# Tile 1's comparisons moved ahead of tile 0's sums, another place for half of a weight, and a changed order of subtractions

## The chip, the cores and the metric

The kernel runs on one core of one Trainium2 chip. The metric is the device time of one execution in microseconds. The core has five engines, each with a queue of its own that it works through in order: TensorE (PE, matrix multiplications), VectorE (DVE), ScalarE (ACT), GpSimd (POOL) and SyncE (SP, which here only issues transfers). An instruction may wait for other engines' work by semaphores, and what stands behind it on its engine then waits too.

## The reference, cut to what matters

An input x of 2048 rows by 512 goes through two branches, mixed by a gate g = sigmoid(x · gate_w):

```python
# branch A: linear attention, 32 heads of 16 features
q, k, v = split(x @ wqkv)
phi_q = concat(softmax(q @ w_phi), softmax(-(q @ w_phi)))     # 32 features a head; phi_k alike
kv, z = phi_k^T @ v, sum(phi_k over rows)
a = ((phi_q @ kv) / (phi_q @ z + 1e-6)) @ wo
# branch B: 32 heads, each picks one of 16 x 16 experts
s1, s2 = (x @ w_q) @ k1, (x @ w_q) @ k2                       # 16 scores each
expert = (argmax(s1), argmax(s2))                             # softmax over one choice is 1
b = sum over heads of gelu(x · u[expert]) * v[expert]
out = g * a + (1 - g) * b
```

What is computed must be seen in one respect: branch B is done by counting. For each row and expert the number of heads that chose it is counted (from the comparisons "score equals the row's largest"), and the counts, multiplied by gelu(x @ u^T), go into one matrix product with v.

## The kernel before, in words

The 2048 rows are 16 tiles of 128. Every float32 product is three products of parts: a number is split into a high part, which a copy rounds, and a low part, the difference (xh and xl for x, wbh and wbl for a weight, and so on).

**First stage** (lines 324 to 579): for each tile the key features, their softmax, the values, and the accumulation of kv (`kvacc`), beside the loading and turning of w_q. From tile 5 on the loop at line 463 takes tiles in pairs t and t+1 and saves products by adding and subtracting parts of x. The rows that matter here, for the pair (t, t+1):
- `x_high` (ScalarE, from tile 3 on) and `x_low` (VectorE, L156) split the tiles t+2 and t+3 before they are needed.
- `k_diffs` (VectorE, four operations L115 to L121) forms a tile's differences to the row's largest and least key feature, reading the product from PSUM; `behind` is the second tile of the pair before, whose differences are made here. `k_exp` (ScalarE L267), `k_sum` (VectorE L271, L272) and `k_mult` (GpSimd L276) finish the softmax.
- `Sums.add(t + 2)` (GpSimd, L175 to L178) adds and subtracts the raw tiles t+2 and t+3 in place, so it must wait until both have been split; `Sums.high` and `Sums.low` (L183, L189) split the results into gh, gl and the places of x15, which TensorE uses in the next pair (`pe`, `pu`).
- Copies of PSUM by ScalarE (L481, L505, L530) start new accumulations from old ones; TensorE waits for them.

**Second stage** (loop at line 944). Pass a does, for tile a, the query features and their softmax (`soft_in`, `soft_exp`, `soft_w`, `soft_sum`, `soft_y`, `soft_p`, `soft_b`); for tile n = a+1, the expert scores (`front_s`, in two halves), the comparisons of each half (`best`: L706 finds each head's largest score, L707 compares) and the transpose of their result by a transfer (`turn_eq`, L713, to `et`); for tile b = a-1, the planes of the softmax that are turned by transfers (`planes`, `join` to `pt`) and the end of the counting; for tile z = a-2 the last products (`back`). `mid_mask(a)` multiplies et with a small matrix (`mk`), from which VectorE counts.

The counting chain (`count`, lines 772 to 808) is a row of some seventeen small VectorE operations on tiles A, B, m, X and T, each of which needs the one before. `step(t, n)` issues n of its links, and so deals them in between other VectorE work; `soft_b` takes a link between each two of its operations, and `dealt` gives five, five and two places between the four operations of the next tile's `soft_in`.

The output weight wo is loaded and split in this stage: two quarters before the loop (`wo_load((0, 1))`), two in pass 0. The high parts are copied by ScalarE (L980), the low parts subtracted by GpSimd (L1006); quarters 0 and 1 go to t1h and t1l, 2 and 3 to the places of the value weights wbh and wbl (quarters 2 and 3 of them), which are free once `vproj(NT - 1)`, the values of the last tile, has been computed in pass 1. The copy of these values (`v15`, L255) releases `kvacc(NT - 1)`.

The order on each engine is the order of the calls in the source, written out by hand. Tiles in pools bring waits: a new tile on an old place waits for that place's last users. The pool `late` holds the key features of every other pair (tag "d", two places) and is closed in pass 1; `w4`, with `pt`, then takes its room.

Of the kernel before, what the change touches and what calls it, by code (L numbers as in the profile page):

```python
# [20 lines left out]
P = 128  # L21
S = 2048
D = 512
# [12 lines left out]
def mix_kernel(ctx, tc, xT, wqT, wkT, wv, wphi, wo, wq, kk, ug, ev, cst, out):  # L36
# [229 lines left out]
    def k_exp(t):  # L266
        act.activation(phis[t], phis[t], AF.Exp)  # L267
# [195 lines left out]
    for t in range(5, NT - 1, 2):  # L463
        n = t + 1
        more = [u for u in (t + 4, t + 5) if u < NT]
        for u in more:
            x_load(u)
        if t == NT - 5:
            rawu = [spare(ug[:, 0:2], "rawu0", [P, 2, NU])]
        elif t == NT - 3:  # L470
            rawu.append(spare(ug[:, 2:4], "rawu1", [P, 2, NU]))
            rawe = [spare(ev[:, 0], "rawe0", [P, D])]
        for u in (t + 2, t + 3):
            if u < NT - 1:
                x_low(u)
        if behind:
            k_diffs(behind)
        a = pks[t] = mm_bank(f"pk{t}")
        prod(a, tile_of(t, 0), b11, True)
        b = mm_bank(f"pu{t}")  # L480
        act.copy(b, a)  # L481
        if 5 < t < NT - 3:
            Sums.add(t + 2)
        if t == 5:
            (j1, tp), = joins
            joins.clear()
            tj1 = wa_.tile([P, D], F32, tag="wtj", bufs=1, name="wtj1")
            join_tp(j1, tp, tj1)
            score_planes(2)
            load_wq()  # L490
            load_wq()
            join_end(j1, tj1)
            Sums.add(t + 2)
        elif t < NT - 3:
            join_all()
        else:
            (j6, tp), = joins
            joins.clear()
            tj6 = wa_.tile([P, D], F32, tag="wtj", bufs=1, name="wtj6")
            join_tp(j6, tp, tj6)  # L500
        e = tr_bank(f"pe{t}")
        prod(e, sums(0, 2), b1, True)
        prod(b, sums(1, 0), b2, False)
        c = mm_bank(f"pv{t}")
        act.copy(c, b)  # L505
        if t == 5:
            k_exp(4)
            k_sum(4)
            k_mult(4)
            join_all()  # L510
        prod(a, tile_of(t, 2), b21, False)
        k_diffs(t)
        if behind:
            k_exp(behind)
            k_sum(behind)
            k_mult(behind)
        score(1)
        if t == NT - 3:
            rawq = stage(wqT, "rawq")
        score(1)  # L520
        for u in (t - 3, t - 2):
            kvacc(u)
        vn, vt = v_tile(n), v_tile(t)
        if t > 5:
            act.copy(vn, by16(e))
            k_exp(t)
            k_sum(t)
        prod(b, sums(0, 0), b3, False)
        d = pks[n] = mm_bank(f"pk{n}")
        act.copy(d, b)  # L530
        if t == 5:
            k_exp(t)
            k_sum(t)
            act.copy(vn, by16(e))
        prod(c, sums(1, 2), b22, False)
        if t == NT - 3:
            x_split(NT - 1)
        dve.tensor_tensor(vt, by16(c), vn, op=ALU.add)
        dve.tensor_tensor(vn, by16(b), vn, op=ALU.add)
        o2 = d.rearrange("p (c n) -> p c n", c=2)  # L540
        prod(o2, tile_of(n, 2), b4, False)
        if t + 3 < NT:
            Sums.high(t + 2)
            Sums.low(t + 2)
        if t == 7:
            for i in range(2):
                x_parts(i, 11)
        for u in more if n < NT - 4 else ():
            x_high(u)
        k_mult(t)  # L550
        behind = n
    t = NT - 1
# [295 lines left out]
        ch, cl, o = st8[t]["c"]  # L848
        eng.tensor_tensor(cl, o[:, :2 * P], ch, op=ALU.subtract)

    woh = [(t1h if k < 2 else wbh)[:, k] for k in range(NK)]
    wol = [(t1l if k < 2 else wbl)[:, k] for k in range(NK)]

    def back_mm(t, cols=slice(0, D), bank=None):
        e = st8[t]
# [43 lines left out]
            pe.matmul(o, neg, zl[:, s_], start=False, stop=True)  # L899
            act.copy(zb[:, s_], o)  # L900

    def wo_load(ks):
        for k in ks:
            rawo[k] = w3.tile([P, D], F32, tag="ot", name=f"rawo{k}")
            sp.dma_start(rawo[k], wo[:, k, :])

    rawo = {}
    kvacc(NT - 2)
# [20 lines left out]
    mid_mask(0)  # L929
    z_final()  # L930
    gelu_rest(0)
    wo_load((0, 1))
    def dealt(a, b, z):
        def first():
            for _ in gate(a):
# [8 lines left out]
    for a in range(NT - 1):  # L944
# [5 lines left out]
            mid_num(z)  # L950
        if a == 2:
            gelu_pre(a)
        if B:
            planes(b, 0)
            if Z:
                c_join(z)
            planes(b, 1)
            front_q(a)
        if owed:
            back(z - 1, owed)  # L960
            store(z - 1)
        if a == 1:
            v15 = vproj(NT - 1)
        gelu_in(a)
        if Z:
            num_lo(z)
        if B:
# [7 lines left out]
        gelu_act(a)  # L975
        if a > 0:
            soft_exp(a)
        if a < 2:
            for k in (2 * a, 2 * a + 1):
                act.copy(woh[k], rawo[k])  # L980
        if Z and not left:
            back(z)
# [17 lines left out]
        soft_sum(a, 0)  # L1000
        soft_sum(a, 1)
        if a == 0:
            step(a, 8)
        if a < 2:
            for k in (2 * a, 2 * a + 1):
                pool.tensor_tensor(wol[k], rawo[k], woh[k], op=ALU.subtract)  # L1006
        if a == 0:
            wo_load((2, 3))
        best(n, 0)
        soft_y(a, 0)  # L1010
        soft_y(a, 1)
        soft_p(a)
        if B:
# [1 line left out]
            gelu_out(b)  # L1015
            coef(b)
            c_planes(b)
        soft_b(a)
        best(n, 1)
        turn_eq(n)  # L1020
        if a != 1:
            gelu_pre(n)
    a, b, z = NT - 1, NT - 2, NT - 3
# [122 lines left out]
```

## Time and profile before

| | |
|---|---|
| median of 3 runs | 376.59 us (376.45 to 376.63) |
| the profiled execution | 376.26 us |
| its span, first to last instruction | 374.5 us |
| TensorE busy | 365.2 us |
| VectorE busy | 334.1 us |
| ScalarE busy | 256.7 us |
| GpSimd busy | 206.3 us |
| bytes read from and written to memory | 26.43 MB, 4.19 MB |

The profile is of one execution. Times are microseconds from its first instruction. A row of the timeline gives the start, the duration, the engine, the line (L56 is line 56), the operation, output and inputs by name, sizes, and how many such operations the row holds; in brackets stands the idle time of the engine ahead of it and what ended it. Durations overlap: a matmul is recorded with 0.39 us, but the next starts 0.23 us after it. A row of the waits gives who waited for what: microseconds in all, times, the longest.

### The profile page before, as it was taken

Reading aid. Unit: us, or ns where it says so; the run is one execution under the profiler, and the core shown is the slowest. Engines: PE = TensorE matmul, PEld = TensorE weight load, DVE = VectorE, ACT = ScalarE, POOL = GpSimd, SP = SyncE. Lnnn points to the kernel's source line nnn. Section 1 sums busy time; section 2 is a strip of 40 time slices with the busy share of each in tenths; the row PEclk is TensorE's granted clock in tenths of the full one; section 3 lists DMA queues with packets and bytes.
Section 4 is the critical chain, followed back from the end, with each engine's and each line's share of the span. In section 5 each row is a group of like instructions: output and inputs, shape, how many; then the busy total and the mean of one; then the engine's idle time right before and its main releaser. Section 6 shows DMA issues by size and latency. Waiting matters only on the chain.

```text
span 374.5 us, 8838 instructions
## 1 busy us (share of the span) xinstructions
PE 365.2 (98%) x3443; PEld 285.7 (76%) x3443; DVE 334.1 (89%) x784; ACT 256.7 (69%) x458; POOL 206.3 (55%) x206
## 2 busy tenths in 40 slices
PE   8999999999999998999999999999999999999995
PEld 4766776667878886778888878888778888888875
DVE  4679898999877989999999999999999999999993
ACT  5576678776576674878759568677786787687741
POOL 1089989799838745844535427335445454454700
PEclk9999999999999999999999999999999999999999
DMA  7967887757981124244253242453553532532201
GB/s 273 330 243 244 302 273 188 255 170 196 265 184 35 21 68 112 45 87 97 71 86 87 70 98 60 98 80 35 113 60 82 114 70 72 115 63 65 72 31 56
DMA packets 72218, 46.67 MB, mean 125 GB/s; under 512 B 63600, under 2 KB 64496, under 8 KB 69872
## 3 DMA queue, kind: packets, MB, share of 16 engines
q1 hardware_dynamic: 71312, 45.24, 47.0%
q10 hardware_dynamic: 864, 0.87, 0.8%
q8 instruction: 27, 0.44, 0.5%
q14 instruction: 15, 0.12, 0.1%
HBM read 26.43 MB, written 4.19 MB: 82 GB/s over the span
## 4 chain that ended last, share of the span: by engine, by line
PE 76%; DVE 7%; ACT 5%; issue 4%; DMA 3%; POOL 3%; POOLq 0%; ACTq 0%; DVEq 0%
PE po L861 10%; PE s L56 6%; PE s L57 6%; PE s L58 6%; PE po L868 5%; PE pq L56 4%; PE pk L453 3%; PE pq L58 3%; PE pq L57 3%; PE ws L292 3%; PE oT L749 2%; PE pu L453 2%; PE kvacc L283 2%; PE pp L57 2%; PE pp L58 2%
## 5 line engine op out<-in xcount | busy, mean ns | idle before, releaser
L663 POOL TENSOR_TENSOR w<-d,zb 128x512 f32<-128x512 f32 x32 | 41.0, 1297 | 78.3 <-ACT d L657 78.3
L56 PE MATMUL s<-sh,xh 128*128 128x512 f32 x128 | 50.8, 397 | 0.0
L57 PE MATMUL s<-sl,xh 128*128 128x512 f32 x128 | 49.9, 390 | 0.0
L58 PE MATMUL s<-sh,xl 128*128 128x512 f32 x128 | 49.8, 389 | 0.0
L698 POOL TENSOR_TENSOR d<-d,st 128x512 f32<-128x512 f32 x30 | 31.2, 1063 | 27.6 <-DVE st L692 25.6
L657 ACT ACTIVATE d<-d 128x512 f32<-128x512 f32 x32 | 20.1, 634 | 32.9 <-DVE d L119 24.8
L276 POOL TENSOR_TENSOR d<-d,st 128x1024 f32<-128x1024 f32 x16 | 33.6, 2101 | 13.3 <-DVE st L272 9.3
L740 ACT COPY pt<-tp 128x1024 uint16<-128x1024 uint16 x28 | 36.3, 1366 | 0.0
L730 ACT COPY pl<-d 128x1024 uint16<-128x1024 uint16 x28 | 29.2, 1045 | 9.1 <-POOL d L698 9.1
L58 PEld LDWEIGHTS s<-sh,xl 128*128 128x128 f32 x128 | 24.0, 188 | 5.0
L56 PEld LDWEIGHTS s<-sh,xh 128*128 128x128 f32 x128 | 24.0, 188 | 4.7
L57 PEld LDWEIGHTS s<-sl,xh 128*128 128x128 f32 x128 | 24.1, 188 | 4.6
L56 PE MATMUL pq<-wah,xh 128*128 128x512 f32 x64 | 26.8, 418 | 0.0
L58 PE MATMUL pq<-wah,xl 128*128 128x512 f32 x64 | 25.1, 392 | 0.0
L57 PE MATMUL pq<-wal,xh 128*128 128x512 f32 x64 | 25.0, 390 | 0.0
L271 DVE TENSOR_REDUCE st<-d 128x64 f32<-128x1024 f32 x16 | 19.4, 1212 | 5.1 <-ACT d L267 4.9
L707 DVE TENSOR_TENSOR eq<-s,mx 128x512 bf16<-128x512 f32 x32 | 22.1, 692 | 1.1
L667 DVE TENSOR_REDUCE st<-d 128x32 f32<-128x512 f32 x32 | 21.6, 683 | 1.6
L267 ACT ACTIVATE d<-d 128x1024 f32<-128x1024 f32 x16 | 17.0, 1065 | 7.6 <-DVE d L121 7.6
L156 DVE TENSOR_TENSOR xl<-xr,xh 128x512 fp32r<-128x512 f32 (+2 forms) x17 | 20.7, 1239 | 1.5 <-ACT xh L152 1.4
L706 DVE TENSOR_REDUCE mx<-s 128x32 f32<-128x512 f32 x32 | 21.8, 682 | 0.0
L677 DVE TENSOR_REDUCE st<-w 128x32 f32<-128x512 f32 x32 | 20.5, 677 | 0.6 <-POOL w L663 0.5
(258 smaller groups left out, 1119.9 us busy)
## 6 DMA issues: line engine op xcount, KB each, us to landing
wq<-wq SPq DMA_DIRECT2D x16, 1024.0 KB, 5.6
xr<-xT SPq DMA_DIRECT2D x15, 256.0 KB, 3.9
y<-ot SPq DMA_DIRECT2D x15, 256.0 KB, 2.3
rawk<-wkT SPq DMA_DIRECT2D x1, 1024.0 KB, 6.0
rawq<-wqT SPq DMA_DIRECT2D x1, 1024.0 KB, 6.7
rawo<-wo SPq DMA_DIRECT2D x4, 256.0 KB, 3.7
rawu<-ug SPq DMA_DIRECT2D x2, 258.0 KB, 4.2
rawv<-wv ACTq DMA_DIRECT2D x2, 256.0 KB, 4.5
```

What stands on the lines that cost most here:

```text
L56: pe.matmul(o, ah, bh, start=(first and i == 0), stop=False)
L57: pe.matmul(o, ah, bl, start=False, stop=False)
L58: pe.matmul(o, al, bh, start=False, stop=(last and i == n - 1))
L276: pool.tensor_tensor(g64(d), g64(d), b64(st[:, 128:192]), op=ALU.mult)
L663: pool.tensor_tensor(hs(e["w"], i), hs(e["ph"], i), hs(zb, i), op=ALU.mult)
L667: dve.tensor_reduce(pair(e["st"][:, 64:128])[:, :, i], hs(e["ph"], i), axis=AX.X, op=ALU.add)
L698: eng.tensor_tensor(g64(d)[:, gs_], g64(d)[:, gs_], r[:, gs_].unsqueeze(2).to_broadcast([P, 32, F]), op=ALU.mult)
L706: dve.tensor_reduce(mx, p3, axis=AX.X, op=ALU.max)
L707: dve.tensor_tensor(e["eq"][:, 512 * half:512 * half + 512].rearrange("p (h f) -> p h f", f=F), p3, mx.unsqueeze(2).to_broadcast([P, H, F] ...
L730: act.copy(pl, e["ph"][:, halves[i]].bitcast(U16).rearrange("p (c j) -> p j c", j=2))
L740: act.copy(p16[:, :, 4 * i:4 * i + 4, :], e["tp"][i].rearrange("p (j g) n -> p j g n", j=2))
L861: pe.matmul(po, a, b, start=(i == 0), stop=False)
```

## The change

Three things change, all of them the order or the place of work; what is computed stays the same.

1. In the pair loop, `k_diffs(behind)` stands ahead of the two `x_low`. For tile 9 alone both splits are taken out of this and moved into the pair (5, 6): the high behind the multiplication of tile 4, the low between the exponential and the sum of tile 5.
2. wo's second half is loaded as one transfer of 512 KB right after the first two quarters, onto a place of the pool `late` that held key features; it is split in pass 1, right after the last tile's values, ahead of `planes` on ScalarE and ahead of `soft_w` on GpSimd, and goes to the first two quarters of wbh and wbl.
3. In pass 0, `best(1, 0)`, `best(1, 1)` and `turn_eq(1)` come earlier, ahead of the sums `soft_y`. Seven links of tile 0's counting chain are dealt around them (3, 2, 2) instead of eight ahead, and `soft_b(0)` takes none, so ten are left for pass 1 where four were.

```diff
-        for u in (t + 2, t + 3):
-            if u < NT - 1:
-                x_low(u)
         if behind:
             k_diffs(behind)
+        for u in (t + 2, t + 3):
+            if u < NT - 1 and u != 9:
+                x_low(u)
...
             k_mult(4)
+            x_high(9)
             join_all()
...
             k_exp(t)
+            x_low(9)
             k_sum(t)
...
         for u in more if n < NT - 4 else ():
-            x_high(u)
+            if u != 9:
+                x_high(u)
...
-    woh = [(t1h if k < 2 else wbh)[:, k] for k in range(NK)]
-    wol = [(t1l if k < 2 else wbl)[:, k] for k in range(NK)]
+    woh = [(t1h if k < 2 else wbh)[:, k % 2] for k in range(NK)]
+    wol = [(t1l if k < 2 else wbl)[:, k % 2] for k in range(NK)]
...
-    def wo_load(ks):
-        for k in ks:
+    def wo_load():
+        for k in range(2):
             rawo[k] = w3.tile([P, D], F32, tag="ot", name=f"rawo{k}")
             sp.dma_start(rawo[k], wo[:, k, :])
+        both = late.tile([P, 2, D], F32, tag="d", name="rawo2")
+        sp.dma_start(both, wo[:, 2:4, :])
+        rawo.update({2: both[:, 0], 3: both[:, 1]})
...
+        if a == 1:
+            front_q(a)
+            v15 = vproj(NT - 1)
+            for k in (2, 3):
+                act.copy(woh[k], rawo[k])
         if B:
             planes(b, 0)
             if Z:
                 c_join(z)
             planes(b, 1)
+        if a > 1:
             front_q(a)
...
+        gelu_in(a)
         if a == 1:
-            v15 = vproj(NT - 1)
-        gelu_in(a)
+            for k in (2, 3):
+                pool.tensor_tensor(wol[k], rawo[k], woh[k], op=ALU.subtract)
...
-        if a < 2:
-            for k in (2 * a, 2 * a + 1):
+        if a == 0:
+            for k in range(2):
                 act.copy(woh[k], rawo[k])
...
         soft_sum(a, 0)
         soft_sum(a, 1)
         if a == 0:
-            step(a, 8)
-        if a < 2:
-            for k in (2 * a, 2 * a + 1):
+            for k in range(2):
                 pool.tensor_tensor(wol[k], rawo[k], woh[k], op=ALU.subtract)
+            step(a, 3)
+        best(n, 0)
         if a == 0:
-            wo_load((2, 3))
-        best(n, 0)
+            step(a, 2)
+            best(n, 1)
+            turn_eq(n)
         soft_y(a, 0)
+        if a == 0:
+            step(a, 2)
         soft_y(a, 1)
         soft_p(a)
...
-        soft_b(a)
-        best(n, 1)
-        turn_eq(n)
+        if a == 0:
+            soft_b(a, lambda t: None)
+        else:
+            soft_b(a)
+            best(n, 1)
+            turn_eq(n)
```

Where the rows come to stand, on the engines concerned. Line numbers of the changed kernel are 3 higher from line 511 on, and up to 19 higher at the end.

VectorE in the first stage, at the end of the pair (5, 6) and the start of (7, 8), before (d_762 and d_806 are the differences of tiles 6 and 7, xr_576 and xr_578 the raw tiles 9 and 10):

```order
L271 TENSOR_REDUCE st_637<-d_636 128x64
L272 RECIPROCAL st_637<-st_637 128x64
L538 TENSOR_TENSOR v_721<-pv_620,v_719 128x32x16
L539 TENSOR_TENSOR v_719<-pu_589,v_719 128x32x16
L156 TENSOR_TENSOR xl_68<-xr_576,xh_65 128x512
L156 TENSOR_TENSOR xl_68<-xr_578,xh_65 128x512
L115 TENSOR_REDUCE st_763<-pk_729 128x32
L117 TENSOR_REDUCE st_763<-pk_729 128x32
L119 TENSOR_TENSOR d_762<-pk_729,st_763 128x32x16
L121 TENSOR_TENSOR d_762<-st_763,pk_729 128x32x16
L115 TENSOR_REDUCE st_807<-pk_768 128x32
```

and now, the same stretch:

```order
L156 TENSOR_TENSOR xl_68<-xr_576,xh_65 128x512
L271 TENSOR_REDUCE st_638<-d_637 128x64
L272 RECIPROCAL st_638<-st_638 128x64
L540 TENSOR_TENSOR v_722<-pv_620,v_720 128x32x16
L541 TENSOR_TENSOR v_720<-pu_589,v_720 128x32x16
L115 TENSOR_REDUCE st_762<-pk_730 128x32
L117 TENSOR_REDUCE st_762<-pk_730 128x32
L119 TENSOR_TENSOR d_761<-pk_730,st_762 128x32x16
L121 TENSOR_TENSOR d_761<-st_762,pk_730 128x32x16
L156 TENSOR_TENSOR xl_68<-xr_578,xh_65 128x512
L115 TENSOR_REDUCE st_807<-pk_768 128x32
```

Tile 9's low has moved ahead of tile 5's sum, and tile 10's behind the differences of tile 6.

VectorE from the end of pass 0 into pass 1, before (st_1750 is tile 0's table of sums and scales, s_1_1821 the second half of tile 1's scores, X and T the counting chain's tiles, pq_1911 tile 1's query features):

```order
L692 SCALAR_TENSOR_TENSOR st_1750<-st_1750,gs_1768 128x32 x2
L802 TENSOR_TENSOR T_1862<-X_1861 128x256
L706 TENSOR_REDUCE mx_1_1890<-s_1_1821 128x32
L707 TENSOR_TENSOR eq_1871<-s_1_1821,mx_1_1890 128x512
L115 TENSOR_REDUCE st_1940<-pq_1911 128x32
L621 RECIPROCAL gs_1895<-gs_1895 128x1
L803 TENSOR_SCALAR X_1861<-T_1862 128x128
L804 TENSOR_SCALAR T_1862<-T_1862 128x128
L805 TENSOR_TENSOR X_1861<-X_1861,T_1862 128x256
L808 TENSOR_TENSOR cf_1946<-X_1861 128x256
L117 TENSOR_REDUCE st_1940<-pq_1911 128x32
```

and now:

```order
L695 SCALAR_TENSOR_TENSOR st_1750<-st_1750,gs_1768 128x32 x2
L115 TENSOR_REDUCE st_1936<-pq_1895 128x32
L624 RECIPROCAL gs_1887<-gs_1887 128x1
L800 TENSOR_SCALAR T_1876<-X_1875 128x256
L801 TENSOR_TENSOR X_1875<-X_1875,T_1876 128x512
L802 TENSOR_SCALAR T_1876<-X_1875 128x256
L803 TENSOR_SCALAR X_1875<-X_1875 128x256
L804 TENSOR_TENSOR X_1875<-X_1875,T_1876 128x512
L117 TENSOR_REDUCE st_1936<-pq_1895 128x32
L805 TENSOR_TENSOR T_1876<-X_1875 128x256
L806 TENSOR_SCALAR X_1875<-T_1876 128x128
```

The second comparison (L706, L707) has left this stretch, and five links of the counting chain stand between L115 and L117 where two and the chain's end stood.

GpSimd in the same stretch, before (d_1749 and d_1939 are the query features of tiles 0 and 1, w their product with z, rawo the loaded quarters of wo):

```order
L1006 TENSOR_TENSOR t1l<-rawo_1812,t1h 128x512
L698 TENSOR_TENSOR d_1749<-d_1749,st_1750 128x512 x2
L625 TENSOR_TENSOR x_1899<-x_1899,px_1898 128x256
L663 TENSOR_TENSOR w_2047<-d_1939,zb 128x32x16 x2
L1006 TENSOR_TENSOR wbl<-rawo_1867,wbh 128x512
L1006 TENSOR_TENSOR wbl<-rawo_1869,wbh 128x512
L635 TENSOR_TENSOR px_1805<-x_1806,px_1805 128x256
```

and now:

```order
L1017 TENSOR_TENSOR t1l<-rawo_1812,t1h 128x512
L701 TENSOR_TENSOR d_1749<-d_1749,st_1750 128x512 x2
L628 TENSOR_TENSOR x_1891<-x_1891,px_1890 128x256
L977 TENSOR_TENSOR wbl<-rawo_1814,wbh 128x512 x2
L666 TENSOR_TENSOR w_2047<-d_1935,zb 128x32x16 x2
L638 TENSOR_TENSOR px_1805<-x_1806,px_1805 128x256
```

The two subtractions for wo have moved ahead of tile 1's products with z.

2 lines of the change are left out of this document (1 added, 1 removed).

## The prediction, made before the changed kernel was timed

> **What bounds the kernel now.** I read the page first (busy times, and the clock granted to TensorE in 40 slices), then TensorE's waits, then the timelines of the engines around those waits.
>
> ```profile
> PE 365.2 (98%) x3443; PEld 285.7 (76%) x3443; DVE 334.1 (89%) x784; ACT 256.7 (69%) x458; POOL 206.3 (55%) x206
> ...
> PEclk9999999999999999999999999999999999999999
> ```
>
> TensorE (PE) is busy for 365.2 of 374.5 us and its instructions are the same in both kernels, in the same order. So the change can gain only where TensorE stands still, and loses wherever it makes TensorE stand longer. The two largest groups of its waits from 40 to 160 us:
>
> ```profile
> PE mk L768 <- DMA et<-eq: 1.6, 1, 1.6
> PE pk L453 <- ACT pk L530: 1.0, 2, 0.6
> ```
>
> So two stretches decide: the pair of tiles 7 and 8 (about 60 to 77 us), and the passage of tiles 0 and 1 in the second stage (about 135 to 156 us). TensorE's timeline in both:
>
> ```profile
> 70.16 0.39 PE L453 MATMUL pv<-wbh,xl 128*128 128x512 f32 x1
> 71.14 0.50 PE L453 MATMUL pk<-sh,xh 128*128 128x512 f32 x1 [0.59 <-ACT pk L530]
> ...
> 74.03 0.39 PE L453 MATMUL pe<-t1h,gh 128*128 128x512 f32 x1
> 74.26 0.39 PE L453 MATMUL pe<-t1l,gh 128*128 128x512 f32 x1
> 74.75 0.50 PE L453 MATMUL pe<-t1h,gl 128*128 128x512 f32 x1
> ...
> 76.00 0.40 PE L453 MATMUL pu<-ul,xh 128*128 128x512 f32 x1
> 76.46 0.50 PE L453 MATMUL pu<-uh,xl 128*128 128x512 f32 x1
> ...
> 148.84 0.36 PE L768 MATMUL mk<-wm,et 128*128 128x16 bf16 x8 [1.61 <-DMA et<-eq]
> 149.13 0.74 PE L283 MATMUL kvacc<-v,d 128*32 128x16 f32 x64
> ...
> 155.37 0.45 PE L749 MATMUL oT<-pt,kvb 64*32 64x128 f32 x16 [0.72 <-ACT pt L740]
> ```
>
> Matmuls of 512 columns start 0.23 apart (74.03 to 74.26), and one after a wait lasts 0.50 instead of 0.39. So the three holes at 71.14, 74.75 and 76.46 cost 0.75, 0.26 and 0.23 us beyond the spacing, and 0.11 more each: 1.57 us.
>
> **Part one: tiles 7 and 8 (lines 473 to 550).** All three holes come from VectorE (DVE) being late.
>
> ```profile
> 55.77 1.94 POOL L276 TENSOR_TENSOR d<-d,st 128x1024 f32<-128x1024 f32 x1
> 55.92 0.68 DVE L121 TENSOR_TENSOR d<-st,pk 128x512 f32<-128x512 f32 x1
> 60.63 0.50 PE L453 MATMUL pe<-t1h,gl 128*128 128x512 f32 x1
> 61.22 3.50 DVE L156 TENSOR_TENSOR xl<-xr,xh 128x512 fp32r<-128x512 f32 x2
> 61.78 2.39 POOL L276 TENSOR_TENSOR d<-d,st 128x1024 f32<-128x1024 f32 x1
> 69.54 1.06 ACT L267 ACTIVATE d<-d 128x1024 f32<-128x1024 f32 x1
> 70.50 0.58 ACT L530 COPY pk<-pu 128x512 f32<-128x512 f32 x1
> ```
>
> Two x lows take 3.50 us ahead of tile 6's differences, so tile 7's exponential starts only at 69.54 and the copy (L530) that TensorE waits for ends at 71.08. With the lows behind, the differences of tile 6 (four operations, 0.6 apart) run from 61.3 to 63.7, x low 10 follows, and tile 7's differences end near 67.4 instead of 69.5. The copy then waits for its matmuls alone, ends near 70.1 and is in time; GpSimd (POOL), fed 2 us sooner, has gl and xl ready more than a microsecond before their matmuls. Gain 1.57. For the two pairs after it VectorE's order changes in the same way, but TensorE has no hole there to win; GpSimd's in-place sums, which must wait for the x lows, move by under half a microsecond against TensorE, and I cost this at nothing: the multiplication of the previous tile covers it.
>
> Tile 9's x high and low move up. The high (0.58, the size of L530, on ScalarE, ACT) falls into a wait for a transposed plane: nothing. The low is issued at 56.6, when tile 5's differences end and GpSimd multiplies until 57.71. The pair of lows above ended at 64.72, 0.55 behind GpSimd's multiplication (64.17), so I take the low to end at 58.26 and GpSimd's next operation to start that much later. Its gl, for which the matmul at 60.63 waits, would slip too, by 0.55 less the idle time GpSimd had ahead of it. Bounds: 0, if GpSimd goes first, and 0.55. I take 0.35. Part one: 0.35 - 1.57 = **-1.2 us** (between -1.6 and -1.0), shifting all that follows.
>
> **Part two: comparisons of tile 1 (lines 1000 to 1022).** Below, times are in the old kernel's clock; the -1.2 is added at the end. The transpose et that TensorE awaits at 148.84 hangs on the second comparison. It moves ahead of both sums and ends near 140.2 (worked out below); the row that follows gives a transpose's time to landing (least, median, most).
>
> ```profile
> DMA to landing us min/median/max: 2.7/2.8/4.6
> ```
>
> So et is there by 145, and the mask matmuls can run 1.78 us sooner, as soon as the matmuls ahead of them are done. That hole closes. But what follows, kvacc at 149.13, needs v15, which ScalarE copies behind the two planes of tile 0, and those wait for GpSimd's scaling (L698). So I follow that chain.
>
> ```profile
> 135.71 0.19 DVE L779 TENSOR_TENSOR sb<-sa 128x64 uint16<-128x64 uint16 x1
> 136.51 0.43 DVE L794 TENSOR_TENSOR X<-m,m 128x256 uint32<-128x256 uint32 x1
> 137.50 2.59 POOL L663 TENSOR_TENSOR w<-d,zb 128x512 f32<-128x512 f32 x2
> 140.04 2.58 POOL L1006 TENSOR_TENSOR t1l<-rawo,t1h 128x512 fp32r<-128x512 f32 x2
> 144.59 2.08 POOL L698 TENSOR_TENSOR d<-d,st 128x512 f32<-128x512 f32 x2 [1.98 <-issue]
> 146.64 0.73 POOL L625 TENSOR_TENSOR x<-x,px 128x256 f32<-128x256 f32 x1
> ...
> 141.32 1.58 DVE L798 TENSOR_TENSOR X<-X,T 128x512 uint16<-128x512 uint16 x1
> 143.79 0.35 DVE L801 TENSOR_TENSOR X<-X,T 128x512 uint16<-128x512 uint16 x1
> 148.76 0.68 DVE L119 TENSOR_TENSOR d<-pq,st 128x512 f32<-128x512 f32 x1
> 154.11 1.22 DVE L685 TENSOR_TENSOR st<-st 128x64 f32<-128x64 f32 x1
> 155.26 0.73 DVE L777 TENSOR_TENSOR sb<-sa 128x64 uint16<-128x64 uint16 x1
> 155.91 0.24 DVE L687 TENSOR_REDUCE st<-st 128x32 f32<-128x96 f32 x1
> 156.08 0.72 DVE L778 TENSOR_TENSOR sa<-sb 128x64 uint16<-128x64 uint16 x1
> ```
>
> Here is what decides. L798 takes 1.58 us beside GpSimd's second t1l, which ends at 142.62; its like L801 takes 0.35 with GpSimd idle. L685, L777 and L778 stretch in the same way, each to the end of the GpSimd operation then running, while the reduction L687 between them does not, nor do reads of PSUM (L119). So a VectorE operation that works from SBUF alone with two tensors, or is a quick one of the counting chain, stands until GpSimd's current operation ends; and as the next link waits for this one, GpSimd's next operation gets in first. With GpSimd back to back, each link costs one GpSimd operation.
>
> The old order put the second comparison and the first reduction of pq, all from PSUM, beside GpSimd's two scalings. In the new one five counting links stand there. The working:
> - Until GpSimd may scale tile 0. From 135.7, where L779 stood: first comparison, two operations of L119's size, 1.3; two links, the second held to the end of the first w (138.8); second comparison to 140.2; first sum of w, 0.65; the m's and X held by both t1l to 142.6, and X's own 0.43: 143.1; second sum, 143.7; six short operations, L672 to L692, at L687's 0.24: 145.2. Scaling at **145.3** instead of 144.59. If X were not held (L794 at 136.51 was not, but began before GpSimd did), it would be 144.3; I take 145.3, since L685 and L777 are of its kind.
> - From there GpSimd has five operations in a row: two scalings (1.04 each), L625 (0.73) and the two wo subtractions (1.28 each, from L1006), whose copies of wbh wait for tile 15's values alone and are done by then. Together 5.4. VectorE's five links fall between them, four adding about 0.2 each, the last 0.28 behind the end: 145.3 + 5.4 + 0.8 + 0.3 = 151.8. Then L117 0.6, the five last links 1.5 without GpSimd (0.3 each, after L801's 0.35), L119 0.7: **154.5**, where the old L119 ended at 149.44.
>
> ```profile
> 149.47 1.23 ACT L657 ACTIVATE d<-d 128x512 f32<-128x512 f32 x2 [0.18 <-DVE d L119]
> 150.61 1.13 ACT L980 CAST wbh<-rawo 128x512 fp32r<-128x512 f32 x2
> 151.64 1.06 ACT L891 COPY kvb<-kvacc 32x128 f32<-32x128 f32 x4
> 152.73 2.58 ACT L740 COPY pt<-tp 128x1024 uint16<-128x1024 uint16 x2
> ```
>
> - ScalarE goes exponentials, kvb, pt; the wo copies (1.03) are gone from between. From the exponential's start to the oT matmuls it was 155.37 - 149.47 = 5.90, now 4.87. So oT's second half comes at 154.5 + 4.87 = 159.4 instead of 155.37: **+4.0 us**, in which the mask hole's gain is already swallowed.
>
> On VectorE the time is partly made up behind this (the wo subtractions no longer hold L685), so the next tiles find their inputs in time and TensorE keeps, but does not add to, the loss.
>
> The Trainium skill ("SBUF — State Buffer", the reading of its diagram) says GpSimd and a VectorE operation with two SBUF inputs or in a two-port mode share one port pair under an exclusive lock, whichever starts first holding it for its whole instruction. By that rule X is held too (scaling at 145.3); by L794's row alone it might not be (144.3, and the loss 3.0). The three holds from 154.11 agree with it.
>
> **Part three: the second half of wo.** One load of twice the size takes the place of two, earlier on SP, ahead of et; it is asked for only when tile 15's values are done, some 13 us later. I cost it at nothing. Moving to wbh's first places changes no count of matmuls. The pt copy must now also wait for the wo subtractions, since pt lies on the loaded tile; they end near 151.5, ahead of it.
>
> **Sum.** -1.2 + 4.0 = +2.8 us. The profiled execution took 376.26 (span 374.5 and 1.76 around it), 0.33 under the median of the runs; 376.26 + 2.8 = 379.1.
>
> **The rivals.**
> - *VectorE is not held.* If its links slipped in between GpSimd's operations at their bare length, scaling would start near 142.5, L119 end near 147.8, and both holes of part two (1.78 and 0.93) close: -1.2 - 2.7 gives 372.4. Against it: three holds in a row at 154.11 to 156.8. For it: L801 and all of the later tiles run free, though there GpSimd idles. If only the first stretch is held and the five links are free, L119 ends near 150.5, oT stays where it was, and part one alone remains: 375.1. The point where it turns: the links may lose 1.2 of the 4.0 us before the gain is gone. Faster in all: 0.20, half for each.
> - *Half held.* Some links meet an idle GpSimd and the loss nearly cancels part one: 376.6. 0.10.
> - *TensorE slows after its long wait.* The wait before oT would be some 4 us long.
>
> ```profile
> 1.10 4.32 PE L344 MATMUL warm<-kvb 128*128 128x384 bf16 x16 [1.10 <-POOL tab L326]
> ```
>
>   At the start, 16 matmuls of 384 columns took 4.32 us, 0.27 each, where 0.17 would follow from 0.23 for 512. If TensorE ran at 0.17 / 0.27 = 0.6 of its rate for as long again after the wait, that would add 0.4 of 4.32, some 1.7 us: 380.8. Against it: the granted clock is full in every slice of the page, after a hole of 1.78 too. 0.10. The Trainium skill ("TensorE: Matmul & The Clock Gate", part 1) has the array drop to half clock after an idle window of about 3.4 us; no wait in this trace is that long.
>
> **How the numbers follow.** A change under 0.2% (0.75 us) can't be told from none. My forecast, slower at 378 to 380, has 0.60; with the slowed clock 0.70 slower, 0.10 the same, 0.20 faster. The range goes from 374.9, which takes in part one alone, to 381.0, past the slow clock; beyond it lie the free links (0.10) and worse holds (0.05). The likeliest case's own range is 378.0 to 380.2.
>
> **What would show it.** Right: no waits of TensorE at 71.14, 74.75 and 76.46; et landing near 143; the five links (lines 800 to 804 of the changed kernel) lasting about a microsecond each beside GpSimd; ScalarE's pt copy late and TensorE waiting 4 us or more for it at oT. Wrong: these links at 0.3 us, or oT without a wait. What would make the total wrong is above all the order in which VectorE and GpSimd take turns.

## The result, and the profile after

The changed kernel is slower: a median of 380.82 us (379.69 to 381.33, four runs) against 376.61 us before, a ratio of 1.0108 (95% interval 1.0084 to 1.0133). That is +4.2 us; the forecast was +2.8 us with 379.1 us, in a range of 374.9 to 381.0. The median lies inside that range, but above the 378.0 to 380.2 that the prediction gave its likeliest case. The profiled execution took 379.69 us with a span of 377.9 us, 3.4 more than before. Of all executions reported below one, of the kernel with part two alone, took 1249 us and is left out.

The same matmuls stand in the same order in both traces, so the loss can be read as a ledger of starts. First the page of the changed kernel, its waits of TensorE, and one stretch of its busy times (us, then busy time and count on PE, weight loads, VectorE, ScalarE, GpSimd, then the granted clock):

```profile
PE 365.3 (97%) x3443; PEld 287.3 (76%) x3443; DVE 334.4 (88%) x784; ACT 256.7 (68%) x458; POOL 205.5 (54%) x206
...
PEclk9999999999999999899999999999999999999999
```

```profile
PE oT L752 <- ACT pt L743: 4.1, 2, 3.3
```

```profile
147.00:160.00 13.00, 8.14 (x125) 6.51 (x126) 12.62 (x30) 8.95 (x22) 7.67 (x9) 0.92 0.28 51
```

No engine does more work. One of 40 slices has a lower granted clock, and in 147 to 160 us TensorE is busy for only 8.14 of 13 us, at a granted clock of 0.92, while VectorE is busy for 12.62. TensorE's timeline, changed kernel, at the places that the prediction showed:

```profile
61.53 0.50 PE L453 MATMUL pe<-t1h,gl 128*128 128x512 f32 x1 [0.82 <-POOL gl L189]
...
71.23 0.39 PE L453 MATMUL pk<-sh,xh 128*128 128x512 f32 x1
...
74.40 0.39 PE L453 MATMUL pe<-t1h,gl 128*128 128x512 f32 x1
...
75.76 0.39 PE L453 MATMUL pu<-uh,xl 128*128 128x512 f32 x1
...
145.90 0.39 PE L58 MATMUL s<-sh,xl 128*128 128x512 f32 x1
146.13 0.36 PE L771 MATMUL mk<-wm,et 128*128 128x16 bf16 x8
147.81 0.74 PE L283 MATMUL kvacc<-v,d 128*32 128x16 f32 x64 [1.32 <-ACT v L255]
...
156.25 0.45 PE L752 MATMUL oT<-pt,kvb 64*32 64x128 f32 x16 [3.31 <-ACT pt L743]
157.46 0.45 PE L752 MATMUL oT<-pt,kvb 64*32 64x128 f32 x16 [0.75 <-ACT pt L743]
...
158.36 0.63 PE L57 MATMUL pq<-wal,xh 128*128 128x512 f32 x1
158.78 0.63 PE L58 MATMUL pq<-wah,xl 128*128 128x512 f32 x1
...
161.34 0.40 PE L58 MATMUL pq<-wah,xl 128*128 128x512 f32 x1
```

And of the kernel before, the last matmul ahead of the mask, which answers to the one at 145.90:

```profile
146.84 0.39 PE L58 MATMUL s<-sh,xl 128*128 128x512 f32 x1
```

Each entry is the changed kernel's start less that of before:

| stretch | us | where it is from |
|---|---|---|
| first 11 us | +0.69 | code that the change leaves alone: the loads of wv came later in this execution |
| pair loop (part one) | -1.63 | from +0.69 to 145.90 - 146.84 = -0.94; the three holes at 71 to 76 are closed, the wait for gl has grown |
| mask to oT (parts two and three) | +3.03 | from -0.94 to 157.46 - 155.37 = +2.09 |
| slow matmuls behind oT | +1.53 | starts 0.43 apart instead of 0.23 until 161.34; by then +3.62 |
| the rest | -0.28 | to +3.34 at the last matmuls, 374.16 and 370.82 |

The chain into oT, as the prediction followed it, on GpSimd, VectorE and ScalarE of the changed kernel:

```profile
144.06 2.13 POOL L701 TENSOR_TENSOR d<-d,st 128x512 f32<-128x512 f32 x2 [2.61 <-issue]
146.15 0.90 POOL L628 TENSOR_TENSOR x<-x,px 128x256 f32<-128x256 f32 x1
147.02 2.61 POOL L977 TENSOR_TENSOR wbl<-rawo,wbh 128x512 fp32r<-128x512 f32 x2
```

```profile
144.51 0.76 DVE L800 TENSOR_SCALAR T<-X 128x256 uint32<-128x256 uint32 x1
145.31 1.17 DVE L801 TENSOR_TENSOR X<-X,T 128x512 uint16<-128x512 uint16 x1
146.50 0.70 DVE L802 TENSOR_SCALAR T<-X 128x256 uint32<-128x256 uint32 x1
147.24 1.25 DVE L803 TENSOR_SCALAR X<-X 128x256 uint32<-128x256 uint32 x1
148.53 1.39 DVE L804 TENSOR_TENSOR X<-X,T 128x512 uint16<-128x512 uint16 x1
...
151.94 0.68 DVE L119 TENSOR_TENSOR d<-pq,st 128x512 f32<-128x512 f32 x1
```

```profile
152.66 1.22 ACT L660 ACTIVATE d<-d 128x512 f32<-128x512 f32 x2 [3.86 <-DVE d L119]
153.79 1.04 ACT L894 COPY kvb<-kvacc 32x128 f32<-32x128 f32 x4
154.85 2.55 ACT L743 COPY pt<-tp 128x1024 uint16<-128x1024 uint16 x2
```

GpSimd runs five operations without a gap from 144.06 to 149.63, and VectorE's five links last until 149.92, each ending just behind the GpSimd operation beside it. ScalarE then waits 3.86 us for L119.

### The profile page after: what moved, and what is told of

Its sections match the earlier page's. It is cut to its first block, busy times and chain, and to the rows that moved or that the text cites. A ratio compares the mean times of both kernels' runs of the same rounds, so it can differ in the third digit from the quotient of the medians.

```text
span 377.9 us, 8836 instructions
## 1 busy us (share of the span) xinstructions
PE 365.3 (97%) x3443; PEld 287.3 (76%) x3443; DVE 334.4 (88%) x784; ACT 256.7 (68%) x458; POOL 205.5 (54%) x206
## 4 chain that ended last, share of the span: by engine, by line
PE 72%; POOL 11%; DVE 7%; ACT 4%; DMA 3%; issue 2%; ACTq 0%; POOLq 0%
PE po L864 10%; PE s L56 6%; PE s L57 6%; PE s L58 6%; PE po L871 5%; PE pq L56 4%; PE pk L453 4%; PE pq L57 3%; PE pq L58 3%; PE pu L453 3%; POOL d L276 3%; PE oT L752 2%; PE ws L292 2%; PE kvacc L283 2%; PE pp L57 2%
## 5 line engine op out<-in xcount | busy, mean ns | idle before, releaser
L276 POOL TENSOR_TENSOR d<-d,st 128x1024 f32<-128x1024 f32 x16 | 32.3, 2017 | 11.3 <-DVE st L272 6.9
L156 DVE TENSOR_TENSOR xl<-xr,xh 128x512 fp32r<-128x512 f32 (+2 forms) x17 | 18.4, 1101 | 1.5 <-ACT xh L152 1.4
```

Source lines behind the costliest of these rows:

```text
L276: pool.tensor_tensor(g64(d), g64(d), b64(st[:, 128:192]), op=ALU.mult)
```

## The experiments

Each kernel was compared with the kernel before in runs taken beside it; gains in us are the ratio times 376.6. Two theories stood at the start. One is the prediction's own: links held by GpSimd make L119 late, and the slow matmuls come from the long wait that follows. The rival has the loss come from elsewhere: the tile 9 move, the wo work, or links that are slow by themselves.

### The pair loop alone, with and without tile 9

The first kernel is the kernel before with part one:

```diff
-        for u in (t + 2, t + 3):
-            if u < NT - 1:
-                x_low(u)
         if behind:
             k_diffs(behind)
+        for u in (t + 2, t + 3):
+            if u < NT - 1 and u != 9:
+                x_low(u)
...
             k_mult(4)
+            x_high(9)
...
             k_exp(t)
+            x_low(9)
             k_sum(t)
...
         for u in more if n < NT - 4 else ():
-            x_high(u)
+            if u != 9:
+                x_high(u)
```

> The kernel before with part one alone: differences ahead of the x lows, tile 9's splits moved. The forecast's step gives -1.2 us, 375.4. Read off the changed kernel's trace, the same stretch gave -0.61 (hole at 57.26), +0.83 (60.63) and -1.76 (71.14 to 83.90), together -1.54: 375.1. Rival: part of that is the late start of that one execution (0.69 us in its first 11 us) made up again, since VectorE and ScalarE had more lead; then the hole at 57.26 comes back and the gain is 0.9: 375.7. The second stage should stand as in the kernel before, its et wait of 1.6 included.

The second swaps `k_diffs` and the lows, but leaves tile 9 where it was.

> As part one, but tile 9's high and low stay in their old place, behind the differences of tile 6 together with tile 10's. If moving the low of tile 9 under GpSimd's multiplication only cost (the wait for gl at 60.63 grew by 0.83), this kernel gains 0.8 more than part one alone: 374.3. If the second low, now ahead of the differences of tile 7, delays these and what hangs on them, the holes at 74.75 and 76.46 stay open (0.23 to 0.26 each, with 0.11 for each start after a wait) and the two are level: 375.1.

Both measured the same: 0.9975 (0.9957 to 0.9994) and 0.9975 (0.9959 to 0.9991), -0.9 us. The holes at 71 to 76 are closed in both, so the swap of the differences does it and tile 9's move has no part in it. The trace of the changed kernel had shown -1.6; what lies beyond -0.9 was given back later in these two kernels. ScalarE's timeline of the kernel with part one alone, then TensorE's:

```profile
104.84 1.38 ACT L308 COPY wtj<-wtp 128x1024 uint16<-128x1024 uint16 x1 [4.58 <-DMA wtp<-wpl]
...
109.92 0.60 ACT L531 COPY pk<-pu 128x512 f32<-128x512 f32 x1
```

```profile
110.58 0.50 PE L453 MATMUL pk<-sh,xh 128*128 128x512 f32 x1 [0.81 <-ACT pk L531]
```

ScalarE stands at L308 until a transposed plane has landed, and what is queued behind it, up to the copy L531, comes late. This plane landed between 100.9 and 104.8 us in the ten executions profiled by the time of the last expectation, and at 106.2 in one after that. In the changed kernel's profiled execution it was early enough (L308 at 103.18), so that trace showed part one at its best. TensorE's gain is real, but it brings TensorE closer to transfers whose time varies.

The price of tile 9's move can be read across executions, since TensorE's holes at 57 and 61 us trade with each other. Their sum is 0.61, 0.93, 0.47 and 0.46 in the four with the old place, and 0.80 to 0.98, mean 0.89, in the nine with the new one. So the move seems to cost some 0.3 us. That is no more than an estimate: one of the four old sums lies among the new ones, and the times of the two kernels above do not differ.

### The links of pass 1 behind L121

```diff
-            soft_in(a, dealt(a, b, z))
+            if a == 1:
+                for _ in gate(a):
+                    pass
+                soft_in(a)
+            else:
+                soft_in(a, dealt(a, b, z))
             drain(b)
```

> The changed kernel, but in pass 1 none of tile 0's ten counting links stands between L115 and L121; all ten follow behind. Theory of the hold: the links beside GpSimd's scalings and wo subtractions still last about a microsecond each, but only their own chain waits for them. L119 ends near 146.0 instead of 152.62, the exponential starts when ScalarE has done its gelu work (148.8), pt follows at 151.0, oT's second half at 153.6 instead of 157.46. TensorE's wait falls from 3.3 to under 1 us, so the half clock behind it goes too: -3.9 -1.6 = -5.5 us, 375.3. Rival: what holds pt back is the wo subtractions or the transposed planes, not L119; then oT stays near 157 and the time near 380.8. Second rival: free links (0.3 each), which this edit would show by their durations.

Measured: 1.0080 (1.0045 to 1.0116), +3.0 us. The first half of the expectation came true, the second did not. TensorE and VectorE of this kernel:

```profile
153.49 1.03 PE L752 MATMUL oT<-pt,kvb 64*32 64x128 f32 x32
...
162.15 0.73 PE L864 MATMUL po<-t1h,xl 128*128 128x512 f32 x2 [2.26 <-DVE xl L763]
```

```profile
151.69 1.40 DVE L804 TENSOR_TENSOR X<-X,T 128x512 uint16<-128x512 uint16 x1
```

oT waits for nothing any more. But the links are still held, six of the ten for 0.7 to 1.4 us, and everything behind them on VectorE slips: tile 1's scaling starts at 160.42 instead of 158.89 (0.7 of this the execution was late already ahead of the mask), and the low parts of oT (L763) come so late that `po` waits 2.26 us, with slow matmuls behind that wait too. The loss has moved one stage on. So it is not a matter of one late instruction: VectorE, busy for 12.62 of 13 us in the changed kernel, has no room there for the held time of ten links, whether ahead of L121 or behind it.

### More work for TensorE in the wait

```diff
     def mid_num(t):
         e = st8[t]
         o = [tr_bank(f"oT{q}_{t}") for q in range(2)]
+        if t == 0:
+            for _ in range(6):
+                pe.matmul(o[0], wah[:, 0, :P], wah[:, 0, :], start=True, stop=True, skip_group_check=True)
```

> The changed kernel with six more matmuls of 512 columns (1.4 us at 0.23) into oT's own bank, ahead of the oT matmuls, where TensorE waited 3.31 us; their result is overwritten. If the half rate of the eight matmuls behind oT (0.43 apart instead of 0.23, 1.57 us in all) comes from the length of the wait, it goes: 379.2, the granted clock 1.00, and the oT matmuls start where they did (156.25 and 157.46). If it comes from anything else (the load on the chip, or the kind of matmul), the time stays at 380.8 and the clock at 0.995 or below.

Measured: 1.0107 (1.0068 to 1.0146), no better than the changed kernel. The second kernel has twelve instead of six.

> The changed kernel with twelve added matmuls instead of six in the wait ahead of oT, 2.8 of its 3.3 us. Six left waits of 1.9 and 0.75 us, 2.6 within 3.4, and the half rate stayed. If the rate depends on how much TensorE idles within a stretch of a few microseconds, and not on one long wait, then with some 0.5 and 0.75 left it goes: clock 1.00, 379.2. If it is set off by something else at that place (the small matmuls at oT), the 0.43 spacing stays and the time is 380.8 or more.

Measured: 1.0045 (1.0023 to 1.0067), granted clock 0.999 to 1.000, which is 2.4 us better than the changed kernel. TensorE with six, then with twelve:

```profile
152.98 1.54 PE L751 MATMUL oT<-wah 128*128 128x512 f32 x6
156.41 0.45 PE L755 MATMUL oT<-pt,kvb 64*32 64x128 f32 x16 [1.89 <-ACT pt L743]
157.61 0.68 PE L755 MATMUL oT<-pt,kvb 64*32 64x128 f32 x16 [0.75 <-ACT pt L743]
...
158.81 0.63 PE L57 MATMUL pq<-wal,xh 128*128 128x512 f32 x1
```

```profile
153.79 2.90 PE L751 MATMUL oT<-wah 128*128 128x512 f32 x12
157.27 0.45 PE L755 MATMUL oT<-pt,kvb 64*32 64x128 f32 x16 [0.58 <-ACT pt L743]
158.47 0.45 PE L755 MATMUL oT<-pt,kvb 64*32 64x128 f32 x16 [0.75 <-ACT pt L743]
...
159.19 0.39 PE L57 MATMUL pq<-wal,xh 128*128 128x512 f32 x1
```

With six, the waits were 1.89 and 0.75 and twelve matmuls behind them ran at half rate, more than without the filling. With twelve, the waits were 0.58 and 0.75 and none did. The oT matmuls are in both, so they do not set it off by themselves. What differs is how long TensorE stands still just ahead of them, and one wait of 3.3 us is not needed. Whether the sum of the waits counts, the longest one, or the work done ahead of them, these two kernels do not separate.

### The old deal of the links, the rest as changed

```diff
-            step(a, 3)
+            step(a, 8)
         best(n, 0)
         if a == 0:
-            step(a, 2)
             best(n, 1)
             turn_eq(n)
         soft_y(a, 0)
-        if a == 0:
-            step(a, 2)
         soft_y(a, 1)
...
-        if a == 0:
-            soft_b(a, lambda t: None)
-        else:
-            soft_b(a)
+        soft_b(a)
+        if a > 0:
             best(n, 1)
             turn_eq(n)
```

> The changed kernel with the old deal of tile 0's links: eight of them ahead of the first comparison, beside an idle GpSimd, five in soft_b, where GpSimd idles too, and four left for pass 1. The comparisons stay sooner and wo stays as changed. Theory: what costs is which links stand beside GpSimd. Four instead of ten in pass 1, each held to the end of one GpSimd operation (about 1.0), so L119 ends near 149.7 instead of 152.62, oT's second half at 149.7 + 4.9 = 154.6 instead of 157.46, TensorE's wait falls to about 1.7 in two parts and the half clock goes: -2.9 -1.6, 376.3. Rival: the comparisons themselves, now ahead of the sums, make VectorE late; then scaling starts near 145.5 instead of 144.06, oT gains less than 1.5 us and the time stays above 378.5.

Measured: 0.9962 (0.9951 to 0.9974), -1.4 us, 5.5 below the changed kernel. This is the experiment that decides: comparisons, wo and pair loop are as changed, and only the place of the links differs. A link of `soft_b`, the last link of pass 1, and TensorE at oT:

```profile
142.39 0.41 DVE L801 TENSOR_TENSOR X<-X,T 128x512 uint16<-128x512 uint16 x1
...
147.46 1.38 DVE L811 TENSOR_TENSOR cf<-X 128x256 f32<-128x256 uint8 x1
```

```profile
153.68 0.45 PE L752 MATMUL oT<-pt,kvb 64*32 64x128 f32 x16 [0.34 <-ACT pt L743]
```

The eight links ahead of the first comparison, most of them beside an idle GpSimd, took 0.17 to 0.42 and the last 0.71, the five in `soft_b` 0.28 to 0.41, and only the four in pass 1 were held (0.48, 0.98, 0.73, 1.38). L119 ended at 150.04 and oT waited 0.34 and 0.75 us. The rival fell: the scaling started at 144.50, hardly later than 144.06.

The next kernel goes on in the same direction. The four links stand behind L121, by the diff of the earlier kernel, and `v15` is copied ahead of the planes:

```diff
-            v15 = vproj(NT - 1)
+            vproj(NT - 1)()
...
-        if a == 1:
-            v15()
```

> As the kernel with the old deal, and beyond it: the four links of pass 1 stand behind L121, and ScalarE copies tile 15's values ahead of the planes. L119 ends near 146.5, kvacc starts at 146.4 without a wait, the chain planes, gelu, exponential, kvb, pt sets oT's second half at 153.8. VectorE's chain is not overloaded as when all ten links were held, since only four are, so nothing comes back in the next pass: 374.5. Rival: the held links only move, and the next tile's oT low parts (L763) are late again, with 1 us or more of wait at po (L864): 376 or more.

Measured: 0.9952 (0.9938 to 0.9967), 374.65 us, -1.8 us: the lowest median of all, below the kernel before by more than the noise. From the kernel ahead of it (0.9962) it can't be told apart. VectorE and TensorE of this kernel:

```profile
145.28 0.67 DVE L119 TENSOR_TENSOR d<-pq,st 128x512 f32<-128x512 f32 x1
...
146.92 1.22 DVE L807 TENSOR_SCALAR T<-T 128x128 uint32<-128x128 uint32 x1
```

```profile
146.72 0.74 PE L283 MATMUL kvacc<-v,d 128*32 128x16 f32 x64
...
153.12 0.45 PE L752 MATMUL oT<-pt,kvb 64*32 64x128 f32 x16 [0.75 <-ACT pt L743]
```

The mask and kvacc wait for nothing, and oT's second half comes at 153.12. The four links are still held there (1.22 us for L807), and oT is not late. So four held links fit into VectorE's time before tile 1's sums, where ten did not; what the earlier copy of `v15` adds was not measured apart.

### GpSimd without the two subtractions

```diff
-        if a == 1:
-            for k in (2, 3):
-                pool.tensor_tensor(wol[k], rawo[k], woh[k], op=ALU.subtract)
```

Here `wol[2]` and `wol[3]` are the high parts, which thus count twice; TensorE's work is the same.

> The changed kernel without the two low parts of wo's second half (GpSimd's L977 in pass 1); the high parts are used in their place, so the output is less exact and TensorE's work the same. Theory of the hold: with GpSimd idle after L628 ends at 147.05, L803 and L804 take 0.3 each instead of 1.25 and 1.39, L802 as before; L119 ends near 150.6 instead of 152.62, oT's second half near 155.4, and the half clock goes as the wait falls to about 1.3 and 0.8: -2.0 -1.6 = 377.2. If links are slow by themselves in this place, the durations stay and so does the time, 380.8.

Measured: 1.0029 (1.0010 to 1.0048), 3.0 us below the changed kernel. The two links on VectorE of this kernel:

```profile
146.92 0.29 DVE L803 TENSOR_SCALAR X<-X 128x256 uint32<-128x256 uint32 x1
147.25 0.42 DVE L804 TENSOR_TENSOR X<-X,T 128x512 uint16<-128x512 uint16 x1
```

They took 1.25 and 1.39 beside the subtractions. L800 to L802, still beside the scalings, kept their 0.76, 1.17 and 0.70. L119 ended at 150.38 instead of 152.62; this execution was 0.3 us ahead already at the mask. So the hold is shown, and its price: 1.93 us for these two links.

### Parts two and three alone

Part three on the kernel before, with the copies and subtractions of the diff above:

```diff
-    wo_load((0, 1))
+    wo_load()
...
-            wo_load((2, 3))
```

> The kernel before with part three alone: wo's second half loaded as one, copied and subtracted in pass 1 ahead of the planes and of tile 1's products with z. The forecast costs the load at nothing and charges the two subtractions to the links beside them. Theory of the hold: four links (803 to 808 in the numbering of the kernel before, which took 0.21, 0.64, 0.29 and 0.42) now stand beside the two subtractions and take about 0.8, 1.25, 1.3 and 0.4, so L119 ends near 151.7 instead of 149.44; the chain behind is 1.03 shorter, so oT's second half comes at 156.5 instead of 155.37: +1.2, 377.8. Rival: the subtractions cost nothing here, and the chain without the copies brings oT 0.9 sooner: 375.7.

Measured: 1.0012 (1.0002 to 1.0022), +0.45 us. The two links beside the subtractions, and TensorE around the mask:

```profile
148.00 1.26 DVE L805 TENSOR_TENSOR X<-X,T 128x256 uint16<-128x256 uint16 x1
149.29 1.39 DVE L808 TENSOR_TENSOR cf<-X 128x256 f32<-128x256 uint8 x1
```

```profile
149.27 0.36 PE L768 MATMUL mk<-wm,et 128*128 128x16 bf16 x8 [1.53 <-DMA et<-eq]
149.56 0.77 PE L283 MATMUL kvacc<-v,d 128*32 128x16 f32 x64
...
151.82 0.63 PE L58 MATMUL s<-sh,xl 128*128 128x512 f32 x1
152.24 0.63 PE L56 MATMUL s<-sh,xh 128*128 128x512 f32 x1
```

Two links are held for 1.94 us more than in the kernel before (0.29 and 0.42 there), and L119 ends at 151.88, where 151.7 was expected, with 0.5 us of this from a later start of the execution. The copies gone from ScalarE (1.03) give half of the hold back, and the time grew by 0.45 where 1.2 was expected. In this execution seven matmuls ran at half rate after a wait of 1.53 us and 1 us of matmuls of 16 columns. They stand ahead of oT, which now starts without a wait; TensorE would otherwise have waited there, so they cost little or nothing.

Part two on the kernel before, with wo as before:

```diff
-            step(a, 8)
...
+            step(a, 3)
         best(n, 0)
+        if a == 0:
+            step(a, 2)
+            best(n, 1)
+            turn_eq(n)
         soft_y(a, 0)
+        if a == 0:
+            step(a, 2)
         soft_y(a, 1)
...
-        soft_b(a)
-        best(n, 1)
-        turn_eq(n)
+        if a == 0:
+            soft_b(a, lambda t: None)
+        else:
+            soft_b(a)
+            best(n, 1)
+            turn_eq(n)
```

> The kernel before with part two alone: comparisons of tile 1 sooner, ten links left for pass 1, wo as before. Theory of the hold: GpSimd has only two scalings and the gelu product (2.8 us) beside the links, so three of the five are held and two run at 0.3 to 0.4. L119 ends near 151.3 instead of 149.44, and with the wo copies still in the chain oT's second half comes at 157.2 instead of 155.37. The et wait (1.78) goes, so TensorE waits some 1.4 at kvacc, then 2.6 and 0.75 at oT, about 3.3 in a few microseconds: the half rate sets in. +1.8 and 1.6: 380. If these waits do not slow it, 378.4. Rival: the subtractions of wo were what hurt, and without them the sooner comparisons gain: below 376.2.

Measured: 1.0104 (1.0063 to 1.0145), +3.9 us. In the profiled execution, the slowest of the three, L797 to L799 took 0.76, 1.17 and 0.70 and the two after them 0.29 and 0.42, as expected. oT waited 2.43 and 0.76 us and its second half came 2.1 us later than before, measured from the matmul ahead of the mask (1.8 expected); twelve matmuls ran at half rate behind it. So part two alone carries nearly the whole loss, and its trace shows both the hold and the half rate. The three parts alone make -0.9 + 3.9 + 0.45 = +3.4 us, the whole change +4.1, which agrees within the intervals.

### ScalarE's wait for the transposed plane

On the kernel with the lowest median, in the pair (13, 14):

```diff
-            join_tp(j6, tp, tj6)
+            tp6 = tp
...
             k_mult(behind)
+        if t == NT - 3:
+            join_tp(j6, tp6, tj6)
```

> The fastest kernel so far (old deal, links behind L121, values of tile 15 first), and in the pair (13, 14) ScalarE's copy of the transposed plane wtp (L308), which waits for a transfer that landed between 100.9 and 104.8 in the executions seen, stands behind the first exponential instead of ahead of the copy L505. If the hole of up to 0.97 us at 110 comes from ScalarE standing behind that transfer, it closes: no wait of TensorE there, 0.3 to 0.9 faster than the kernel without this edit, 374.0. Rival: the tail of ScalarE's work there (two exponentials, three copies) is the limit anyway, and nothing changes: 374.6.

Measured: 0.9961 (0.9947 to 0.9976), no better than without the edit. The hole at 110 was not there, but one of the same kind stood in the pair (9, 10): TensorE waited 0.80 us at 84.63 for ScalarE's copy, behind a plane that had come late. With one profile each, whether the edit helps at its own place can't be told from chance; this stays open.

## Why the prediction was right in kind, and where its sizes were off

**Part one.** Forecast -1.2, measured alone -0.9, and -1.6 in the changed kernel's execution. All three holes closed, as worked out. Tile 9's 0.35 fits the estimate of some 0.3, which is not firm. The sum left out the hole at 57.26, which trades with that at 61, and the waits behind transposed planes at 84 and 110, which take back up to a microsecond.

**Part two, the hold.** The mechanism was as described: five links of 0.70 to 1.39 us, ending with GpSimd's operations; and taking away two of GpSimd's operations gave two links back their bare length. The Trainium skill ("SBUF — State Buffer", the reading of its diagram) gives the exclusive lock for it; the 0.29 instead of 1.25 us of L803 agrees. The runs show the hold and its price; they do not show by what the two engines get in each other's way. The size was too large by 1.0: +4.0 forecast, +3.03 measured. In the old kernel's clock (add the 0.94 of the table) the scaling started at 145.0, not 145.3, and the five links ended at 150.86, not 151.8. The step that failed is the term "four adding about 0.2 each": GpSimd ran back to back, so a link's start gap lies inside the next GpSimd operation and adds nothing. These 0.8 are most of the miss; the scaling was 0.3 early and GpSimd's five operations 0.2 longer (5.57 instead of 5.4). From there L117 to L119 took 2.8 and ScalarE 4.84 to oT, as forecast.

**"TensorE keeps, but does not add to, the loss".** This was wrong in that execution: 1.53 us more were lost to half rate. The rival "TensorE slows after its long wait" came true with nearly its size (1.7); it had a chance of 0.10, and the sum stood without it. Of the +2.8 forecast, without the start's 0.69 the measured terms would be -1.63 + 3.03 - 0.28 = +1.1; the half rate makes up the rest. So the total came near through two errors of opposite sign, which is luck: the hold was put too high, and the half rate at nothing. The other three runs of the changed kernel had granted clocks of 0.990, 0.991 and 0.994 instead of 0.995 and took 0.8 to 1.6 us more, which may be why the median lies above the profiled execution; only one was profiled. By medians the twelve added matmuls took 2.4 of the 4.1 us away, which suggests that the half rate mostly cost more than the 1.53 of the trace. The median ended at the figure of that rival, 380.8, and not at the forecast's 379.1.

**Against the slow clock** the prediction held that the clock was full after a hole of 1.78. That row was true and proved too little: at the same hole seven matmuls slowed in the execution with part three alone. The Trainium skill ("TensorE: Matmul & The Clock Gate", part 1) names an idle window of about 3.4 us. The wait of 3.31 us is near it, but those of 1.53, and of 1.89 and 0.75, are well short of it, and here the measurement decides: half rate set in behind them too.

**Part three at nothing.** The load cost nothing, as said, but alone the part costs 0.45 us: the subtractions hold whatever links stand beside them. Inside the change the sum had charged them to part two, so the total is not affected.

**The signs to look for.** No waits at 71, 74 and 76, links of about a microsecond, the late pt, a wait of 4 us (3.31 and 0.75): all seen. et landed near 144.3 rather than 143, since its transfer took 5.2 us instead of 2.8; TensorE did not wait for it.

## What to carry to other kernels

Where VectorE and GpSimd both work from SBUF, look up for each small VectorE operation what GpSimd does beside it. Here a read of PSUM (L119) took 0.67 us beside GpSimd's scaling and 0.68 without it, and the two reductions L667 of the kernel before took 1.28 and 1.26, while links of 0.28 to 0.42 us grew to as much as 1.4; so such a short dependent chain goes where GpSimd idles. Taking a held chain out of the critical path helped with four held links and not with ten: where the engine has no room for the held time, the wait comes back a stage later. Before moving work into a stage where TensorE will wait, add the price of the half rate that may follow.

## What the runs showed that was not expected

TensorE's half rate needs no long wait. It followed a wait of 3.31 us (with 0.75 behind it), of 2.43 and 0.76, of 1.89 and 0.75, of 2.26 and 0.37, and of 1.53 with small matmuls behind it; it did not follow 0.58 and 0.75, nor the 1.61 ahead of the mask in the kernel before. So no length of wait as such divides these cases. It lasted some 3 to 5 us at 0.43 instead of 0.23 between matmuls of 512 columns, 1.4 to 2.6 us lost, and half-rate matmuls ahead of another wait cost little: the kernel before had a granted clock of 0.995 in 15 of the 51 executions beside the experiments, and by their medians these differed from the others of their group by -0.3, +0.1 and +0.4 us. The kernel without the two subtractions waited 1.36 and 0.75 us; seven of its ten executions had a granted clock of 0.994 or 0.995 and took 377.2 to 379.0 us, and the three at 0.998 to 1.000 took 375.8 to 376.1. So the same kernel shows both, chance has a part in it, and a kernel with such waits can vary by 2 us and more from run to run.
